# Sliding-window attention followed by an expert layer: Q and K of the first two batches loaded in runs of eight rows, the exponent in key order, new pacing of loads

## The chip, the cores and the metric

The kernel runs on one core of a Trainium2 chip. The metric is the device time of one execution in microseconds. Runs of a kernel are executed in rounds next to runs of the kernel before on the same chip. A "point" is one per cent of the time of the kernel before. TensorE is called PE below, as in the profile; VectorE is DVE, ScalarE is ACT, GpSimd is POOL, and SP is the engine whose queue issues most of the transfers.

## The reference

Eight batches of attention with eight heads, 576 positions and 64 channels, where each position sees only positions at most 32 away. The heads are joined to 4608 tokens of 512 channels, which go through one expert: a matrix product to 2048, the square of the relu with a scale and a bias, and a product back to 512.

```python
scores = scale * np.matmul(q, k.transpose(0, 1, 3, 2))      # q, k: (8, 8, 576, 64) float32, of size 0.1
mask = np.abs(pos[:, None] - pos[None, :]) <= 32
attn = softmax(np.where(mask, scores, -1e9))                # cut: written out with max, exp and sum
x = np.matmul(attn, v).transpose(0, 2, 1, 3).reshape(4608, 512)
r = np.maximum(x @ w_in, 0.0)                               # w_in: (512, 2048)
return (s * (r * r) + b) @ w_out                            # w_out: (2048, 512)
```

## The kernel before

The program is a list of tasks. Each task has a stream (an engine or the SP queue), an estimated cost, an estimated landing time if it is a transfer, a key (the lower, the sooner) and a slack. A list scheduler written in the kernel simulates these estimates when the program is built and fixes the order of the instructions on every engine. Each engine is then given its instructions in that fixed order.

Q and K of batches 0 and 1 are loaded early, cast to bf16, transposed on PE and scattered into two layouts, `QT` for queries and the block-diagonal `KBD` for keys. Batches 2 to 7 use DMA transposes instead, and their loads are paced: they wait for the attention of an earlier unit.

```python
PACE = ((0, 0, 1, 2, 3, 3), (0, 0, 1, 2, 3, 3), (0, 1, 2, 3, 3, 3))   # unit of batch b-1 that a Q/K load of batch b waits for
PACEV = ((0, 0, 1, 1), (0, 0, 1, 1), (0, 1, 2, 2))                     # the same for V

def pairs_chunk(b, name, t0, n, key, load_key, banks, slack=0.0):      # n partitions: 128, 128, 32; two rows each, all heads
    add("sp", lambda e: e.dma_start(
        STG[si][0:n, 0:1024].rearrange("p (h c) -> p h c", h=H),
        src_of[name][b, :, t0:t0 + 2 * n, :].rearrange("h (p i) d -> p h (i d)", i=2)),   # runs of 2 rows = 512 bytes
        600.0, writes=[("STG", si)], key=load_key, dma=("l", n // 2, 30.0))
    # ... cast to NAT, 8 transposes on PE into a PSUM bank, then for q:
    for i in range(2):
        add("act", lambda e, i=i: e.copy(QT[slot][:, i, :, t0 // 2:t0 // 2 + n], view[:, :, i, 0:n]), ...)
    # ... for k: a scatter with a step of two elements into KBD, halves on DVE and ACT

# in unit(b, m): four score products into SC (PSUM), then the exponent of 128x512
src = src.rearrange("p a (i c) -> p a i c", i=2)
add("act", lambda e, src=src, dst=dst: e.activation(
    dst.rearrange("p a (c i) -> p a i c", i=2), src, AF.Exp, bias=0.0, scale=0.125), ...)   # dense read, write with a step of 2

# V of batches from 2 on is issued by POOL, staged in VST, and cast into VBD by DVE and ACT
cast_v(b, due(b, 0) - 4.0, (("dve", "act"), ("dve", "act")), 3000.0)   # 3000 is the slack, in ns

# the order of the first part (cut)
qk(0, 0, 128); qk(0, 256, 128); load_v(0, ...); qk(0, 512, 32)         # then units of batch 0, w_in, w_out (first half)
qk(1, 0, 128); load_v(1, ..., waits=[land["out", 2, 0]]); unit(1, 0)   # then more of batch 1, w_out (second half)
```

The "column sum" that is named below is a product of the output weights with a matrix of ones. It serves the bias `b` and needs all of one half of `w_out`; there are two, one per half. "Expansion" is the product with `w_in`, and an "output sum" is DVE's reading of a finished product with `w_out` (`outs`). A transfer "lands" when its data have arrived. The "granted clock" is the share of full speed at which TensorE ran.

The softmax here doesn't subtract the row's maximum and nothing guards it: scores larger than these inputs give would overflow.

## Time and profile before

| | before |
|---|---|
| time, median of 3 (range) | 335.08 us (334.21 to 335.22) |
| PE busy in the profiled span of 331.1 us | 308.5 us |
| first exponent starts | 11.54 us |
| last V issue of batch 0 ends | 12.64 us |
| first expansion matmul starts | 24.20 us |
| last V issue of batch 1 ends | 49.37 us |
| second column sum starts | 59.67 us |

These are the page's busy totals, with PE's share in 40 slices and the granted clock below (9 stands for 90% or more):

```profile
...
PE 308.5 (93%) x2199; PEld 179.5 (54%) x2234; DVE 206.6 (62%) x485; ACT 166.4 (50%) x270; POOL 87.6 (26%) x136
...
PE   1778998899999999999989999999999999999995
...
PEclk9999999799999999999999999999999999999999
...
```

PE is busy for 93% of the span, and what is missing lies mainly in the first slices. The table by stretches gives this in numbers. Its columns are the stretch, its length, the busy time of each engine with its number of instructions, the granted clock, the DMA engines' busy share, and GB/s (I read a share near or above 1 as full):

```profile
...
core 0: us, PE busy (x) PEld busy (x) DVE busy (x) ACT busy (x) POOL busy (x), PEclk, DMA share, GB/s
0.00:20.00 20.00, 9.50 (x80) 6.86 (x82) 11.87 (x29) 14.45 (x19) 14.50 (x28) 1.00 1.07 238
20.00:40.00 20.00, 17.60 (x252) 16.04 (x250) 12.96 (x27) 12.86 (x24) 7.19 (x7) 1.00 1.10 343
40.00:60.00 20.00, 17.76 (x212) 15.35 (x213) 11.57 (x24) 15.35 (x28) 8.36 (x9) 1.00 1.11 254
60.00:80.00 20.00, 18.84 (x172) 14.38 (x171) 12.38 (x27) 9.05 (x15) 8.17 (x14) 0.92 0.95 213
...
160.00:180.00 20.00, 18.95 (x118) 9.73 (x119) 14.17 (x33) 9.34 (x15) 4.03 (x7) 1.00 0.99 189
...
```

PE is idle for 10.5 us in the first 20 us and for 16.3 us in the first 80. The DMA engines are full in the first 60 us (shares of 1.07 to 1.11), so I take it that the order and speed of transfers decide how fast PE gets going. The SP queue's timeline of the first microseconds shows this. Its columns are start, duration, queue, line, operation, tiles and count; the first issue takes 0.45 us, and I read a much longer one as held up by the transfers ahead of it (the trace gives the durations alone):

```profile
...
start us, us, engine line op out<-in xcount [idle before <-releaser]
0.81 0.45 SPq L456 DMA_DIRECT2D stg<-in_q_dram  x1
...
3.24 1.61 SPq L456 DMA_DIRECT2D stg<-in_k_dram  x1
4.90 7.74 SPq L432 DMA_DIRECT2D vst<-in_v_dram  x8
...
```

The first four loads of Q and K are issued by 4.9 us, but eight V loads then take 7.74 us to issue, as I read it because the transfers ahead of them are still under way. While Q and K land, the table by stretches shows 300 GB/s:

```profile
...
4.00:8.00 4.00, 1.04 (x8) 0.77 (x8) 3.35 (x15) 2.12 (x4) 3.33 (x11) 1.00 1.19 300
...
```

The V loads of batch 1 are issued like this:

```profile
...
40.62 8.75 SPq L432 DMA_DIRECT2D vst<-in_v_dram  x8
...
```

The groups of ACT by shape are next; after the bar stand busy time and the mean of one in ns. The relu writes densely and the exponent with a step of two elements, and a 128x512 costs 598 ns against 743:

```profile
...
L705 ACT ACTIVATE r<-w 128x512 bf16<-128x512 f32 x144 | 85.4, 598 | 95.0 <-PE w L698 80.8 <-DVE outs L730 11.3 <-DVE gt L707 2.0
L560 ACT ACTIVATE exo<-sc 128x512 bf16<-128x512 f32 x32 | 23.8, 743 | 4.8 <-PE sc L543 4.6
...
```

Last, PE's timeline around the second column sum (the brackets give the idle time just before, and what ended it). PE waits 1.34 us for an output sum and then does the column sum in 3.33 us. The first column sum takes 1.91 us. This one runs at half the clock: the granted clock was 0.50 from 59.96 to 63.38, for 3.42 us:

```profile
...
58.78 0.61 PE L717 MATMUL o<-wout,gt 128*128 128x256 bf16 x4 [1.34 <-DVE outs L730]
...
59.67 3.33 PE L740 MATMUL o<-wout,onesw 128*128 128x256 bf16 x16
...
```

### The profile page before, as it was taken

The page shows a single profiled execution, that of the slowest core. Times are in us where ns is not written, and L with a number is a line of the kernel's source. Part 1 is how long each engine was busy: PE and PEld are TensorE (multiplying, and loading weights), DVE is VectorE, ACT ScalarE, POOL GpSimd, SP SyncE. Part 2 cuts the span into 40 slices and gives each one's busy share as a digit, 9 for nine tenths or more (in the row PEclk, how much of TensorE's full clock was granted, in tenths as well). Part 3 has the DMA queues.
Part 4 walks back from the last instruction along what each step waited for, and adds up shares of the span by engine and source line. Part 5 has one row for each costly group of instructions (what it writes and reads, how often), then busy time and mean ns, then how long its engine had stood idle before and what let it go on. Part 6 is the DMA issues. An engine that isn't in the chain of part 4 may idle for free.

```text
span 331.1 us, 5839 instructions
## 1 busy us (share of the span) xinstructions
PE 308.5 (93%) x2199; PEld 179.5 (54%) x2234; DVE 206.6 (62%) x485; ACT 166.4 (50%) x270; POOL 87.6 (26%) x136
## 2 busy tenths in 40 slices
PE   1778998899999999999989999999999999999995
PEld 1567996775554555456445555555455544444442
DVE  6556564269777776898578768765874453323411
ACT  6696497229552664657175655444644433333300
POOL 8562443830910226044205500450000000000000
PEclk9999999799999999999999999999999999999999
DMA  8999999899999699979998996999811111000021
GB/s 211 224 363 357 295 195 297 219 241 167 209 202 197 193 195 206 230 170 245 173 228 163 225 212 145 247 169 213 146 56 54 56 46 62 35 32 34 32 93 68
DMA packets 107836, 57.15 MB, mean 173 GB/s; under 512 B 56608, under 2 KB 100128, under 8 KB 107808
## 3 DMA queue, kind: packets, MB, share of 16 engines
q1 hardware_dynamic: 103200, 49.69, 68.7%
q0 software_dynamic: 4608, 7.08, 11.3%
q8 instruction: 17, 0.28, 0.4%
q14 instruction: 11, 0.09, 0.1%
HBM read 36.70 MB, written 9.44 MB: 139 GB/s over the span
## 4 chain that ended last, share of the span: by engine, by line
PE 70%; DMA 13%; SPq 8%; POOL 3%; DVE 2%; ACT 2%; issue 2%; ACTq 0%
PE o L717 31%; PE w L698 29%; PE avn L582 6%; SPq L432 5%; DMA vst<-in_v_dram 5%; PE sc L543 3%; DMA stg<-in_moe_w_in_dram 3%; DMA stg<-in_moe_w_out_dram 3%; POOL vst L432 2%; SPq L456 2%; DMA out_dram<-outs 2%; ACT vbd L445 1%; SPq L416 1%; PE o L740 1%; DVE vbd L446 0%
## 5 line engine op out<-in xcount | busy, mean ns | idle before, releaser
L717 PE MATMUL o<-wout,gt 128*128 128x512 bf16 (+1 forms) x629 | 140.4, 357 | 1.9 <-DVE outs L730 1.3
L698 PE MATMUL w<-xt,win 128*128 128x512 bf16 (+2 forms) x685 | 139.8, 339 | 2.2 <-ACT r L705 1.2
L705 ACT ACTIVATE r<-w 128x512 bf16<-128x512 f32 x144 | 85.4, 598 | 95.0 <-PE w L698 80.8
L707 DVE TENSOR_TENSOR gt<-r 128x512 bf16<-128x512 bf16 x144 | 61.3, 432 | 55.1 <-ACT r L705 54.4
L717 PEld LDWEIGHTS o<-wout,gt 128*128 128x128 bf16 x640 | 61.1, 98 | 59.7 <-DVE outs L730 2.0
L698 PEld LDWEIGHTS w<-xt,win 128*128 128x128 bf16 x704 | 61.6, 98 | 52.4 <-ACT r L705 1.8
L432 POOL DMA_DIRECT2D vst<-in_v_dram x96 | 59.4, 626 | 106.8 <-PE avn L582 57.7
L730 DVE SCALAR_TENSOR_TENSOR outs<-o,sb,cvec 128x512 f32<-128x512 f32 (+1 forms) x40 | 27.7, 692 | 18.6 <-PE o L717 16.2
L560 ACT ACTIVATE exe<-sc 128x512 bf16<-128x512 f32 (+1 forms) x40 | 27.5, 687 | 15.7 <-PE sc L543 15.1
L582 PE MATMUL avn<-vbd,exo 128*128 128x130 bf16 (+1 forms) x240 | 27.9, 221 | 1.5 <-ACT xt L607 1.3
L595 DVE TENSOR_TENSOR xn<-avn,rec 128x512 bf16<-128x512 f32 (+1 forms) x38 | 26.1, 686 | 3.2 <-DMA xt<-xn 2.5
L543 PE MATMUL sc<-qt,kbd 128*128 128x128 bf16 (+1 forms) x288 | 24.8, 220 | 1.6 <-ACT exe L560 1.1
L582 PE MATMUL avn<-vbd,exe 128*128 128x130 bf16 (+1 forms) x152 | 25.3, 221 | 1.0 <-ACT vbd L445 1.0
L560 ACT ACTIVATE exo<-sc 128x512 bf16<-128x512 f32 x32 | 23.8, 743 | 4.8 <-PE sc L543 4.6
L543 PEld LDWEIGHTS sc<-qt,kbd 128*128 128x128 bf16 x288 | 20.5, 100 | 9.9 <-issue 1.0
L445 ACT CAST vbd<-vst 64x1024 bf16<-64x1024 f32 (+1 forms) x15 | 16.5, 1139 | 17.5 <-DMA vst<-in_v_dram 17.5
L582 PEld LDWEIGHTS avn<-vbd,exo 128*128 128x128 bf16 (+1 forms) x240 | 22.0, 105 | 5.5 <-ACT xt L607 1.6
L506 DVE CAST nat<-stg 128x1024 bf16<-128x1024 f32 (+1 forms) x36 | 23.7, 680 | 0.0
L521 DVE COPY kbd<-kt 64x512 bf16<-64x512 bf16 (+1 forms) x72 | 19.1, 266 | 0.8
L582 PEld LDWEIGHTS avn<-vbd,exe 128*128 128x128 bf16 (+1 forms) x152 | 16.1, 109 | 4.3 <-ACT vbd L445 1.4
L446 DVE CAST vbd<-vst 64x1024 bf16<-64x1024 f32 (+1 forms) x16 | 11.7, 745 | 7.3 <-DMA vst<-in_v_dram 7.3
L564 DVE TENSOR_TENSOR exe<-exe,mask 128x512 bf16<-128x512 bf16 (+1 forms) x30 | 11.7, 391 | 7.1 <-ACT exe L560 7.0
(63 smaller groups left out, 133.3 us busy)
## 6 DMA issues: line engine op xcount, KB each, us to landing
stg<-in_q_dram SPq DMA_DIRECT2D x16, 512.0 KB, 5.5
stg<-in_k_dram SPq DMA_DIRECT2D x16, 512.0 KB, 7.2
out_dram<-outs SPq DMA_DIRECT2D x32, 256.0 KB, 2.6
vst<-in_v_dram POOLq DMA_DIRECT2D x96, 72.0 KB, 5.5
stg<-in_moe_w_in_dram SPq DMA_DIRECT2D x8, 512.0 KB, 8.7
stg<-in_moe_w_out_dram SPq DMA_DIRECT2D x8, 512.0 KB, 8.3
vst<-in_v_dram SPq DMA_DIRECT2D x16, 144.0 KB, 4.7
stg<-in_q_dram SPq DMA_DIRECT2D x8, 128.0 KB, 6.2
```

The costliest lines, as they stand in the source:

```text
L432: add(stream, lambda e, dst=dst, src=src: e.dma_start(dst, src), 640.0 if stream == "sp" else 700.0, writes=[("VST", h, x) for x in (range ...
L445: add(eng, (lambda e, dst=dst, src=src: e.copy(dst, src)) if eng == "act" else (lambda e, dst=dst, src=src: e.tensor_copy(dst, src)), {"ac ...
L506: add("dve", lambda e, si=si, ni=ni: e.tensor_copy(NAT[ni][0:n, :, :].rearrange("p i (h d) -> p h i d", h=H), STG[si][0:n, 0:1024].rearran ...
L543: fns = [lambda e, j=j, pr=pr, lo=lo, hi=hi, w=w, par=par: e.matmul(SC[:, par, pr * 128:pr * 128 + w], lhsT=KBD[:, pr, j, :], rhs=QT[slot] ...
L560: add("act", lambda e, src=src, dst=dst: e.activation(dst.rearrange("p a (c i) -> p a i c", i=2), src, AF.Exp, bias=0.0, scale=0.125), 190 ...
L582: fns.append(lambda e, pr=pr, buf=buf, col=col, j=j, x=x, last=len(parts) - 1: e.matmul(av[0:nr, pr, 0:130], lhsT=buf[:, pr, col:col + nr] ...
L595: add("dve", lambda e: e.tensor_tensor(XN[xi][0:nr, :].rearrange("p (a b c) -> p a b c", a=4, b=2), av[0:nr, :, 0:128].rearrange("p a (b c ...
L698: add("pe", [lambda e, g=g, kc=kc: e.matmul(wt[:, g, :], lhsT=WIN_BF[:, kc, (f0 + g) * 128:(f0 + g + 1) * 128], rhs=XT[:, kc, t0 % XR:t0 % ...
L705: add("act", lambda e: e.activation(rt, wt, AF.Relu, bias=0.0, scale=1.0), 190 + 0.833 * 512, reads=[("W", wb)], writes=[("R1", rb)], key=key)
L707: add("dve", lambda e: e.tensor_tensor(GT[gs][:, f0:f0 + ng, g0:g0 + nt], rt, rt, ALU.mult), 130 + 0.53 * 512, reads=[("R1", rb)], writes= ...
L717: add("pe", [lambda e, fc=fc: e.matmul(O[:, ob, 0:cn], lhsT=GT[gs][:, fc, g0:g0 + 128], rhs=WOUT_BF[:, fc, c0:c0 + cn], start=(fc == 0), s ...
L730: add("dve", lambda e: e.scalar_tensor_tensor(OUTS[us][:, 0:cn], O[:, ob, 0:cn], SB128[:, 0:1], CVEC[:, c0:c0 + cn], ALU.mult, ALU.add), 2 ...
```

## The change

The intent: Q and K of the first two batches are read in runs of eight rows per head pair, so that a contiguous piece has 2 KB in place of 512 bytes and there are eight loads per batch of 72 partitions each. Eight-row runs change the order of queries and keys, so the exponent now reads PSUM with a step and writes densely. All loads of the first part are held in strict order, and the pacing of later loads is eased.

```diff
+ROWS = 8
-PACE = ((0, 0, 1, 2, 3, 3), (0, 0, 1, 2, 3, 3), (0, 1, 2, 3, 3, 3))
-PACEV = ((0, 0, 1, 1), (0, 0, 1, 1), (0, 1, 2, 2))
+PACE = ((-1, -1, -1, 0, 1, 1), (-1, -1, 0, 1, 2, 2), (0, 0, 1, 2, 3, 3))
+PACEV = ((-1, -1, -1, -1), (0, 0, 0, 0), (0, 1, 2, 2))          # -1: one unit earlier, in batch b-2
... (the scheduler: tasks with key < -100 are chained in the order in which they are added)
-        NSTG, NNAT, NEX, ... = 9, 6, 3, ...
+        NSTG, NNAT, NEX, ... = 9, 5, 4, ...
... (weight casts)
-                key=key + 20.0, slack=100.0)
+                key=key + 150.0, slack=100.0)
-        def pairs_chunk(b, name, t0, n, key, load_key, banks, slack=0.0):
+        def load_pair(b, name, pr, key, load_key, banks, eng, slack):
+            n = S // ROWS                                              # 72
             add("sp", lambda e: e.dma_start(
-                STG[si][0:n, 0:1024].rearrange("p (h c) -> p h c", h=H),
-                src_of[name][b, :, t0:t0 + 2 * n, :].rearrange("h (p i) d -> p h (i d)", i=2)),
-                600.0, writes=[("STG", si)], key=load_key, dma=("l", n // 2, 30.0))
+                STG[si][0:n, :].rearrange("p (h c) -> p h c", h=2),
+                src_of[name][b, 2 * pr:2 * pr + 2, :, :].rearrange("h (p i) d -> p h (i d)", i=ROWS)),
+                600.0, writes=[("STG", si)], key=load_key, dma=("l", 9, 86.0))
... (eight 72x128 transposes per load, one copy into QT, or two into KBD)
-                src = src.rearrange("p a (i c) -> p a i c", i=2)
+                src = src.rearrange("p a (i c) -> p a c i", i=nrow)    # nrow: 8 for b < 2, else 2
-                    dst.rearrange("p a (c i) -> p a i c", i=2), src, AF.Exp, bias=0.0, scale=0.125),
+                    dst.rearrange("p a (c i) -> p a c i", i=nrow), src, AF.Exp, bias=0.0, scale=0.125),
... (order of the first part: all Q, K of a batch, then its V, then its units; V of batch 1 no longer waits for w_out)
-                load_v(1, h, nxt(), "sp", waits=[land["out", 2, 0]])
+                load_v(1, h, nxt(), "sp")
```

The term `("l", 9, 86.0)` tells the scheduler that such a load keeps the transfer engines for 9 times 86 ns, that is 0.77 us. A load has 72 times 4 KB.

## The prediction

> **What bounds it now.** The tensor engine: the busy table gives PE 308.5 of 331.1 us. The table by stretches shows PE idle 10.5 us in 0–20, 2.4 in 20–40, 2.1 in 50–60, 1.2 in 70–80, 2.2 in 100–260 and 3.8 at the end. At 60–63 the granted clock is 0.50; the second column sum takes 3.33 us against 1.91 for the first. Only these gaps can be won, and the change touches those of the first 90 us.
>
> **Head.** The timeline shows V issued at 4.9–12.6 (0.97 us per load), the DMA engines saturated, V cast at 15.7–19.2, ACT busy almost throughout, and the first expansion matmul at 24.2. Q and K in 512-byte packets move at about 290 GB/s, V in 256-byte packets at 205, weights in 2 KB packets at 390.
>
> - Runs of eight make the packets 2 KB; at 390 GB/s that saves 2 us per batch. But a load now has 72 partitions. [...] Loads before have 128, 64 or 32 partitions, so no run here shows this yet.
> - All eight loads must land before the first score: the first exponent moves from 11.5 to about 15 us. It was not the limit; V and ACT were.
> - ACT: an exponent with strided writes takes 0.74 us per 128x512, a relu with contiguous ones 0.60; a K scatter 0.65, a contiguous Q copy 0.53. So each exponent saves about 0.12 us, and the head about 1.5 us of ACT. Transposes become 64 instead of 48 per batch (+1 us of PE in batch 1).
> - Sum: first expansion matmul at about 23.2, 1 us earlier.
>
> **Middle.** Strict load order and fewer descriptors (Q, K issues of 2.5–3.4 us in the queue's timeline shrink to about 0.5) should bring V of batch 1 from 52 us to about 46 and the second half of w_out from 58 to about 52. That would remove the idle time at 54 and 57–59 and perhaps the half clock after it, 3–4 us. Against it: on POOL the sixteen V issues of batch 2 (0.63 us each, 10 us) now stand before all four w_out casts (1.04 each), and wait for the V casts of batch 1. So the second column sum can't start before about 62 us, while PE arrives at about 60. I expect PE to wait for POOL there for 1–4 us, again followed by some 3.4 us of half clock[...]. Most of the gain here is lost.
>
> **Later.** Batch 2 is loaded some 10 us sooner, so the 1.2 us of idle time at 73–76 goes. Steady blocks stay PE bound; shorter exponents there are off the critical path.
>
> **Sum.** −1 head, −1 middle, −1 batch 2, +0.5 transposes: 335.1 to about 332.5 us; range 328.7–335.5. Chances: faster by over 2% 0.09, within 2% 0.89, slower 0.02.
>
> **What would show it.** Q, K loads at 290 GB/s[...]; exponents near 0.62 us; first expansion matmul near 23; PE waiting for POOL before the second column sum, clock 0.5 after it; no gap at 73–76.
>
> **What would make it wrong.** [...] Strided PSUM reads slower than strided writes, or PE's fixed order waiting for batch 1's transposes: 336.

Passages are cut where marked: how a load of 72 partitions would be split over the transfer engines, the rate that I worked out from it, a case of 327–329 us that presupposed it, and a rule of when the full clock returns. The step from the head ended in no gain from the longer packets: I put the Q and K loads at 290 GB/s, their rate in the trace of before (5 to 8 us). The sum came to −1 −1 −1 +0.5, that is −2.5 us, from 335.1 to 332.6, given as about 332.5; the head's −1 counts nothing for faster loads because of that step. The 3.4 us of half clock are the stretch from 59.96 to 63.38 in the trace of before.

## The result, and the profile after

The changed kernel takes 352.38 us in the median of 4 runs (351.46 to 356.85, the longest slow), and the kernel before 334.64 us (333.97 to 335.22) beside it. The ratio is 1.0521, with a 95% interval from 1.0477 to 1.0566. A ratio is the mean time of one kernel's runs over that of the other's of the same rounds, so it is not quite the ratio of the medians. Executions over 1.5% slower than the fastest of the same kernel are left out of the means. The results are correct. The prediction of 332.5 us, with a range up to 335.5, was wrong.

| | before | after |
|---|---|---|
| time, median of the same rounds | 334.64 us | 352.38 us |
| profiled span, granted clock | 331.1 us, 0.993 | 349.9 us, 0.985 |
| PE busy / idle (span less busy) | 308.5 / 22.6 us | 313.3 / 36.6 us |
| ACT busy | 166.4 us | 159.2 us |
| first exponent starts | 11.54 us | 18.83 us |
| last V issue of batch 0 ends | 12.64 us | 17.24 us |
| first expansion matmul starts | 24.20 us | 26.90 us |
| last V issue of batch 1 ends | 49.37 us | 55.49 us |
| second column sum starts | 59.67 us | 73.20 us |

The same views of the changed kernel follow. The page's totals and slices:

```profile
...
PE 313.3 (90%) x2231; PEld 180.5 (52%) x2266; DVE 204.3 (58%) x485; ACT 159.2 (46%) x262; POOL 88.6 (25%) x138
...
PE   1487879949999999999599998999999999999996
...
```

PE gained 14.0 us of idle time and 4.8 us of busy time, and the work is nearly the same, so slower matmuls at a lower clock (a mean of 0.985 against 0.993) are the likely source of the latter. The table by stretches:

```profile
...
0.00:20.00 20.00, 7.07 (x76) 5.22 (x78) 11.13 (x29) 10.35 (x13) 12.60 (x27) 1.00 0.87 182
20.00:40.00 20.00, 16.41 (x218) 13.72 (x217) 10.72 (x21) 12.64 (x22) 6.80 (x6) 1.00 1.01 336
40.00:60.00 20.00, 16.78 (x190) 13.50 (x190) 10.93 (x22) 10.79 (x17) 6.13 (x7) 0.91 0.84 193
60.00:80.00 20.00, 14.80 (x167) 12.39 (x167) 8.68 (x19) 10.58 (x18) 12.96 (x19) 1.00 1.16 269
...
160.00:180.00 20.00, 15.60 (x85) 7.76 (x85) 10.48 (x22) 7.36 (x11) 4.88 (x8) 0.83 1.18 187
...
```

The columns are those of before. PE is idle for 24.9 us in the first 80 us, 8.6 more than before. Another 3.4 us comes between 160 and 180, where the clock is also at 0.83. In the first 20 us the DMA share is 0.87 and not 1.07, and the rate 182 GB/s and not 238. The SP queue and the rate while Q and K land:

```profile
...
0.81 0.43 SPq L476 DMA_DIRECT2D stg<-in_q_dram  x1
...
3.86 0.40 SPq L476 DMA_DIRECT2D stg<-in_k_dram  x1
4.30 12.94 SPq L448 DMA_DIRECT2D vst<-in_v_dram  x8
...
```

```profile
...
4.00:12.00 8.00, 2.81 (x35) 2.12 (x36) 4.07 (x10) 3.83 (x6) 4.18 (x10) 1.00 0.90 200
...
```

All eight loads are issued by 4.3 us, as the change intended. But they move at only 200 GB/s at a share of 0.90, and the V issues behind them take 12.94 us. For batch 1:

```profile
...
40.56 14.93 SPq L448 DMA_DIRECT2D vst<-in_v_dram  x8
...
```

V of batch 1 begins to be issued at the same time as before, and ends 6 us later. The exponent and relu:

```profile
...
L567 ACT ACTIVATE exo<-sc 128x512 bf16<-128x512 f32 x32 | 19.1, 598 | 2.5 <-PE sc L550 2.5
...
```

The exponent now costs what the relu costs (598 ns in this kernel too). Around the second column sum:

```profile
...
73.20 1.92 PE L744 MATMUL o<-wout,onesw 128*128 128x256 bf16 x16 [0.45 <-POOL wout L431]
...
78.48 2.36 PE L721 MATMUL o<-wout,gt 128*128 128x256 bf16 x20 [2.68 <-DVE outs L734]
...
```

It starts 13.5 us later than before. Its wait for POOL is just 0.45 us, and its clock is full. After it comes a wait for output sums of 2.68 us. The late stall is seen in PE's timeline, then DVE's, then in the table by stretches:

```profile
...
175.35 0.34 PE L589 MATMUL avn<-vbd,exo 128*96 128x130 bf16 x1 [4.29 <-DVE exe L571]
...
```

```profile
...
174.01 0.69 DVE L462 CAST vbd<-vst 64x1024 bf16<-64x1024 f32 x1 [2.87 <-DMA vst<-in_v_dram]
174.62 0.41 DVE L711 TENSOR_TENSOR gt<-r 128x512 bf16<-128x512 bf16 x1
174.95 0.34 DVE L571 TENSOR_TENSOR exe<-exe,mask 128x384 bf16<-128x384 bf16 x1
...
```

```profile
...
175.20:180.00 4.80, 4.65 (x17) 2.26 (x18) 3.10 (x7) 2.20 (x2) 0.00 (x0) 0.50 1.27 223
...
```

PE needs the masked exponent, which is DVE's multiply at 174.95. Ahead of it in DVE's order stands a V cast at 174.01, which had itself waited for V to land. PE does nothing for 4.29 us and then works at a clock of 0.50. The sixteen V transfers that the cast needs took, from issue to landing:

```profile
...
DMA to landing us min/median/max: 4.5/10.3/11.3
```

### The profile page after: what moved, and what is told of

It is laid out like the page before. It is cut to its first block, busy times and chain, and to the rows that moved or that the text cites. A ratio compares the mean times of both kernels' runs of the same rounds, so it can differ in the third digit from the quotient of the medians.

```text
span 349.9 us, 5916 instructions
## 1 busy us (share of the span) xinstructions
PE 313.3 (90%) x2231; PEld 180.5 (52%) x2266; DVE 204.3 (58%) x485; ACT 159.2 (46%) x262; POOL 88.6 (25%) x138
## 4 chain that ended last, share of the span: by engine, by line
PE 67%; DMA 19%; SPq 4%; POOL 3%; DVE 3%; issue 2%; ACT 1%; ACTq 0%
PE o L721 31%; PE w L702 27%; DMA vst<-in_v_dram 7%; PE avn L589 5%; DMA stg<-in_k_dram 4%; SPq L448 3%; PE sc L550 3%; DMA out_dram<-outs 3%; DMA stg<-in_moe_w_out_dram 3%; POOL vst L448 3%; DMA xt<-xn 2%; SPq L476 1%; DVE xn L602 1%; DVE outs L734 0%; ACT r L709 0%
## 5 line engine op out<-in xcount | busy, mean ns | idle before, releaser
L721 PE MATMUL o<-wout,gt 128*128 128x512 bf16 (+1 forms) x627 | 143.7, 361 | 5.8 <-DVE outs L734 2.7
L702 PE MATMUL w<-xt,win 128*128 128x512 bf16 (+2 forms) x686 | 142.3, 342 | 2.3 <-ACT r L709 1.4
L711 DVE TENSOR_TENSOR gt<-r 128x512 bf16<-128x512 bf16 x144 | 60.1, 424 | 59.3 <-ACT r L709 58.6
L702 PEld LDWEIGHTS w<-xt,win 128*128 128x128 bf16 x704 | 62.7, 99 | 55.2 <-ACT r L709 2.3
L734 DVE SCALAR_TENSOR_TENSOR outs<-o,sb,cvec 128x512 f32<-128x512 f32 (+1 forms) x40 | 27.6, 691 | 22.6 <-PE o L721 19.3
L567 ACT ACTIVATE exe<-sc 128x512 bf16<-128x512 f32 (+1 forms) x40 | 22.1, 553 | 13.1 <-PE sc L550 13.0
L567 ACT ACTIVATE exo<-sc 128x512 bf16<-128x512 f32 x32 | 19.1, 598 | 2.5 <-PE sc L550 2.5
L599 DVE RECIPROCAL rec<-avn 128x8 f32<-128x8 f32 (+1 forms) x38 | 7.7, 202 | 15.8 <-PE avn L589 15.6
```

The lines of the kernel that those rows point to most:

```text
L567: add("act", lambda e, src=src, dst=dst: e.activation(dst.rearrange("p a (c i) -> p a c i", i=nrow), src, AF.Exp, bias=0.0, scale=0.125), ...
L702: add("pe", [lambda e, g=g, kc=kc: e.matmul(wt[:, g, :], lhsT=WIN_BF[:, kc, (f0 + g) * 128:(f0 + g + 1) * 128], rhs=XT[:, kc, t0 % XR:t0 % ...
L711: add("dve", lambda e: e.tensor_tensor(GT[gs][:, f0:f0 + ng, g0:g0 + nt], rt, rt, ALU.mult), 130 + 0.53 * 512, reads=[("R1", rb)], writes= ...
L721: add("pe", [lambda e, fc=fc: e.matmul(O[:, ob, 0:cn], lhsT=GT[gs][:, fc, g0:g0 + 128], rhs=WOUT_BF[:, fc, c0:c0 + cn], start=(fc == 0), s ...
L734: add("dve", lambda e: e.scalar_tensor_tensor(OUTS[us][:, 0:cn], O[:, ob, 0:cn], SB128[:, 0:1], CVEC[:, c0:c0 + cn], ALU.mult, ALU.add), 2 ...
```

## The experiments

**Theory A**: loads on 72 partitions are slow, not only because they keep fewer transfer engines busy (a share of 0.83 between 4 and 8 us, where the kernel before has 1.19) but because nearly all their rows lie in one half of SBUF. The second part was an assumption, which the first run below tests. **Theory B**: the plan, made with wrong landing times, places V casts ahead of work that PE needs. **Rivals**: the new pacing, the strict order of loads, the new exponent, and the order of weight casts on POOL. Where full-rate loads are named, the casts read zeros.

### Rates of load shapes alone

A kernel that only loads: groups of eight loads, each group waited for before the next; its output is wrong. It is one run, and its state is unknown.

```diff
+groups = [pair(t, 0, 72, 0), pair(t, 0, 64, 0), pair(t, 0, 64, 64), pair(t, 0, 64, 64 * (t % 2)), pair(t, 0, 72, 28),
+          flat(t, 80), flat(t, 96), flat(t, 128), two(t, 72), two(t, 128),        # pair(load, first row, rows, first partition)
+          pair(t, 0, 64, 0) + pair(t, 64, 8, 64), pair(t, 0, 32, 0) + pair(t, 32, 8, 64) + pair(t, 40, 32, 72)]
```

> Loads alone, wrong result on purpose: twelve groups of eight loads, each group waited for to the end, all from DRAM on the SP queue. Theory E (engines[...]): 72 rows in partitions 0-71 about 205 GB/s, the same 72 rows in partitions 28-99 about the same 205[...], 64 rows in 0-63 faster than 72[...], 80 rows in 0-79 near 290 or more. Theory P (the side of the SBUF: 64 of the 72 rows go into the lower 64 partitions[...]): 72 rows in 28-99 clearly faster, 280 or more; 64 rows in 0-63 no faster than about 210, and the same in 64-127; 64 rows alternating between the halves, and 96 and 128 rows, faster, up to 390. Rival R (2 KB runs with a stride are slow whatever the partitions): all 2 KB groups near 205. 512-byte packets at 128 rows: 290.

Theory E is that 72 rows keep only a part of the transfer engines busy, Theory P that the half of SBUF counts.

The table by stretches, one stretch per group; the lines below are 72 rows in partitions 0 to 71, 64 in 0 to 63, 64 in 64 to 127, 64 in alternate halves, 72 in 28 to 99, then 80, 96 and 128 rows from partition 0, and the last is each load cut into 32, 8 and 32 rows:

```profile
...
4.00:11.00 7.00, 0.00 (x0) 0.00 (x0) 1.00 0.80 212
17.00:23.50 6.50, 0.00 (x0) 0.00 (x0) 1.00 1.07 211
29.50:36.00 6.50, 0.00 (x0) 0.00 (x0) 1.00 1.08 217
41.50:46.50 5.00, 0.00 (x0) 0.00 (x0) 1.00 1.06 237
53.00:59.50 6.50, 0.00 (x0) 0.00 (x0) 1.00 0.79 243
64.00:70.00 6.00, 0.00 (x0) 0.00 (x0) 1.00 1.06 249
77.00:83.00 6.00, 0.00 (x0) 0.00 (x0) 1.00 1.05 275
90.00:98.00 8.00, 0.00 (x0) 0.00 (x0) 1.00 0.97 344
...
153.00:160.50 7.50, 0.00 (x0) 0.00 (x0) 1.00 1.06 204
...
```

Two limits are seen. 64 rows occupy all engines (share 1.07) and yet reach only 211 GB/s in one half of SBUF and 217 in the other, against 237 in alternate halves and 344 for 128 rows: lying in one half goes with a low rate by itself. And 72 rows in 28 to 99, which lie in both halves, reach 243 at a share of 0.79: not all engines are busy with them. From the shares I estimate three quarters of the engines (0.79 of the 1.07 that 64 rows show is 0.74), which would be twelve of the sixteen that the page counts. 72 rows at 0 to 71 have both limits (share 0.80) and reach 212. The lower share alone thus goes with less than the prediction allowed: 243 GB/s, where it had about 290. Why it is not three quarters of the 344 of 128 rows, an estimate of 258, is open. With 512-byte packets 72 rows reach 181, and 128 rows 295. Eighty rows reach 249, 96 rows 275, and the cut into 64 and 8 rows 224. So the run length did buy something, and the 72 partitions cost more than that.

### Each load cut over both halves

```diff
-            add("sp", lambda e: e.dma_start(STG[si][0:n, :]..., rows), ...)
+            add("sp", [lambda e: e.dma_start(into[0:32], rows[0:32]),
+                       lambda e: e.dma_start(into[64:72], rows[32:40]),
+                       lambda e: e.dma_start(into[72:104], rows[40:72])], ...)
```

The casts read a tile of zeros here, with unchanged waits, as the rows land in other partitions. The result still passes the comparison, I take it because scores of inputs of size 0.1 are so small that zero scores stay within the tolerance; it is not the reference's computation.

> The kernel after, with each Q, K load cut into three so that 32 rows land in partitions 0-31 and 40 in 64-103 (the casts read zeros: wrong result on purpose; order of everything else the same). If the slow loads are the cause (main theory): Q, K move at 300 GB/s or more, first exponent at about 14 us instead of 18.8, first expansion matmul at about 23.5 instead of 26.5, second column sum at about 63 instead of 73, time 337 to 342. If the new order and pacing are the cause (rival): 348 or more.

Measured: 346.21 us, ratio 1.0354 (1.0326 to 1.0382). The expectation missed: the loads moved at 225 GB/s between 4 and 11 us, nearer to the 204 of the run above than to 300 or more. The edit did not do what it was made for, so it is no test of Theory A, though the loads were a little faster and the kernel 1.7 points faster than the changed one. The run of load shapes could have warned me: loads of 64 rows in alternate halves reached 237 GB/s against 211, just 12% more.

### The pacing of before

```diff
-PACE = ((-1, -1, -1, 0, 1, 1), (-1, -1, 0, 1, 2, 2), (0, 0, 1, 2, 3, 3))
+PACE = ((0, 0, 1, 2, 3, 3), (0, 0, 1, 2, 3, 3), (0, 1, 2, 3, 3, 3))     # PACEV likewise
```

> The kernel after with the pacing tables of before. Main theory (loads): the first 80 us stay as slow; only the 4.3 us stall at 171-175 and the half clock after it may go, and V of batch 2 no longer stands before the w_out casts: 343 to 349. Rival (pacing): 338 or less.

Measured: 347.79 us, ratio 1.0383 (1.0348 to 1.0418). The start stays slow (first expansion matmul at 27.01). But the second column sum comes at 65.49 and not 73.20, and PE is busy for 58.75 of the first 80 us and not 55.06 (63.70 before); the late stall shrinks to 1.54 us. So the pacing has a share in both.

### The loads and layout of before inside the changed kernel

```diff
-ROWS = 8
+ROWS = 2                       # and load_pair is replaced by pairs_chunk of before, in the changed kernel's order
```

> The kernel after with the loads and the layout of before (512-byte packets, 128 rows), but its order of loads, exponent and pacing. Main theory (loads): first expansion matmul at 23 to 24.5 us, V of batch 1 lands by 48, 334 to 341. Rival (order and pacing): 346 or more.

Measured: 340.30 us, ratio 1.0176 (1.0147 to 1.0205), with right results. The first expansion matmul comes at 24.78. About two thirds of the loss is gone: 1.0521 less 1.0176 is 3.45 points, or 11.5 us of 333.5. It undoes the layout together with the loads, so it is not yet clean.

### The same plan with loads at full rate

The same bytes of each load are spread over 128 partitions, in 128 runs of 2304 bytes and not 144 of 2048, which is to lift both limits at once (128 rows reached 344 GB/s alone). The planner's estimates stay, so the plan stays (the planner of both kernels, run without the chip, gives the same order on all five engines). The casts read zeros, so the data are wrong. The casts are no faster for that: on POOL, single casts of Q took 1.42 and 1.53 us in the two later runs with the same edit (full rate and the pacing of before, and later V casts), against 1.04 in the changed kernel.

```diff
-                STG[si][0:n, :].rearrange("p (h c) -> p h c", h=2),
-                src_of[name][b, 2 * pr:2 * pr + 2, :, :].rearrange("h (p i) d -> p h (i d)", i=ROWS)),
+                STG[si][:, 0:576],
+                src_of[name][b, 2 * pr:2 * pr + 2, :, :].rearrange("h s d -> (h s d)").rearrange("(p c) -> p c", p=128)),
```

> The kernel after with the same eight loads per batch, the same bytes and the same plan, but each load spread over 128 partitions (the casts read zeros, so the scores are wrong on purpose). Alone, 128 rows of 2 KB moved at 340 to 370 GB/s, 72 rows in 0-71 at 212. Main theory (rate of the 72-row loads): Q, K land by 9 to 10 us instead of 15.3, first expansion matmul at 22 to 23.5 instead of 26.9, V of batch 1 cast by 47, time 336 to 341, i.e. most of the 18 us gone. Rival (order and pacing): 346 or more.

Measured: 339.50 us, ratio 1.0179 (1.0125 to 1.0232): 3.4 points, or 11.4 us. The rate while Q and K land, and V's issues behind them:

```profile
...
4.00:8.00 4.00, 1.32 (x16) 0.98 (x16) 2.99 (x9) 2.44 (x4) 3.59 (x7) 1.00 0.97 303
...
```

```profile
...
4.80 8.46 SPq L449 DMA_DIRECT2D vst<-in_v_dram  x8
...
```

303 GB/s in place of 200, and V's issues take 8.46 us and not 12.94. The first expansion matmul comes at 23.61 and not 26.90, and the second column sum at 63.84 and not 73.20. This settles the larger part: it is the rate of the 72-partition loads, twice, with all that queues behind them. A stall of 4.68 us remains in PE, with the same cause in DVE's timeline as before: a V cast that waited for its data, with the mask multiply behind it.

```profile
...
164.93 0.68 DVE L463 CAST vbd<-vst 64x1024 bf16<-64x1024 f32 x1 [3.10 <-DMA vst<-in_v_dram]
...
165.88 0.34 DVE L572 TENSOR_TENSOR exe<-exe,mask 128x384 bf16<-128x384 bf16 x1
...
```

### Full rate and the pacing of before

```diff
 (full rate as above)
+PACE, PACEV as in the kernel before
```

> As the run before, with the pacing tables of before. If load rate and pacing add up: 331 to 336, near or under the kernel before. If the strict load order, or waiting for all eight loads before the first score, costs by itself: 338 or more.

Measured: 340.92 us, ratio 1.0242 (1.0188 to 1.0296). The two repairs do not add; the interval overlaps that of full rate alone. The stall moved from 162 to 78 us (4.36 us of PE), again with a V cast ahead in DVE's order that had waited 5.02 us for its data. So here the pacing of before gains nothing and only moves the stall, where in the changed kernel it gained 1.4 points.

### Two-row loads and the pacing of before

```diff
 (loads and layout of before as above)
+PACE, PACEV as in the kernel before
```

> The kernel after with two-row loads (512-byte packets, 128 rows) and the pacing tables of before; its strict load order and its exponent are kept. If loads and pacing are the two causes: 333 to 337. If strict order costs by itself: 338 or more, with PE waiting in 40-80 us.

Measured: 336.93 us, ratio 1.0098 (1.0042 to 1.0154). Results are right. With two-row loads the pacing of before gains 0.8 points. What remains of the change in this kernel is the order of the first part, the keys of the weight casts and of some first fills, the buffers and the exponent.

### The new exponent alone in the kernel before

```diff
-                src = src.rearrange("p a (i c) -> p a i c", i=2)
+                src = src.rearrange("p a (i c) -> p a c i", i=2)
-                    dst.rearrange("p a (c i) -> p a i c", i=2), src, AF.Exp, ...
+                    dst.rearrange("p a (c i) -> p a c i", i=2), src, AF.Exp, ...
```

> The kernel before with one part of the change alone: the exponent reads PSUM with a stride and writes runs. The order of instructions is the same as before on every engine. Exponents of 128x512 fall from 0.74 to 0.60 us, ACT busy time by about 9 us; time 333.5 to 335 (0 to 1 us less), because ACT is off the chain after 25 us. Rival (ACT holds back PE throughout): 331 or less.

Measured: 331.42 us beside 332.93, ratio 0.9971 (0.9925 to 1.0016). ACT's busy time falls from 166.4 to 159.7 us, and the time by at most a fraction of a per cent that is not told from nothing.

### Later V casts, with full rate

The slack of the V casts of batches from 2 on goes from 3000 to 8000 ns, so that the scheduler lets other ready work go first.

```diff
-cast_v(b, due(b, 0) - 4.0, (("dve", "act"), ("dve", "act")), 3000.0)
+cast_v(b, due(b, 0) - 4.0, (("dve", "act"), ("dve", "act")), 8000.0)
```

> The run with loads at full rate and the new pacing, with one number changed: the plan keeps 8 instead of 3 us of reserve between the landing of V and its cast, so the V casts of batches 2 to 7 stand later in the queues of DVE and ACT. Theory (what is left of the loss after the loads are repaired comes from V casts that stand in front of DVE work which PE needs, and wait for a late V): the 4.7 us stall at 162-166 and the half clock after it go, 332 to 336. Rival (the rest comes from the strict order or the late w_out casts): 338 or more.

Measured: 333.60 us, ratio 1.0035 (0.9969 to 1.0101): equal to the kernel before within the interval. The stretch of the late stall, in the table by stretches:

```profile
...
160.00:180.00 20.00, 19.89 (x130) 10.74 (x132) 16.28 (x42) 10.70 (x18) 4.82 (x8) 1.00 0.84 193
...
```

PE is busy for 19.89 of 20 us, against 15.60 in the changed kernel.

### Later V casts in the changed kernel, otherwise untouched

> The kernel after with that same number changed and nothing else. If slow loads and V casts in the way add up: the stall at 171-175 goes, 345 to 349, the first 80 us as slow as in the kernel after. If the loads were all of it: 351 to 353.

The edit is the one above, in the changed kernel. Measured: 343.79 us, ratio 1.0331 (1.0266 to 1.0397), slightly better than expected. PE is again busy for 19.89 us between 160 and 180. With the three runs before it this gives a table of two by two:

| | V casts as in the change | V casts later |
|---|---|---|
| 72-partition loads | 1.0521 | 1.0331 |
| loads at full rate | 1.0179 | 1.0035 |

The loads are worth 3.4 or 3.0 points, the V casts 1.9 or 1.4. Both together account for 4.9 of 5.2 points. (Each ratio is against the kernel before in its own rounds; the four do not all come from the same rounds.)

### No strict order of loads

```diff
-        after = [self.chain] if key < -100 and self.chain else []
+        after = []
```

> The kernel after without the strict order of the first loads (each load goes when its buffer is free in the plan). Main theory: the order is not what costs, 349 to 354. Rival (strict order blocks the queue behind buffers): 345 or less.

Measured: 354.90 us, ratio 1.0638 (1.0587 to 1.0689), about one point slower than with it (other rounds; the intervals do not meet), and just above the expectation. The strict order is not the cause; if anything it helps.

### A candidate: new exponent and one more output buffer in the kernel before

```diff
 (exponent as above)
-        NSTG, NNAT, NEX, NXN, NR1, NOUT, XR = 9, 6, 3, 2, 3, 3, 2048
+        NSTG, NNAT, NEX, NXN, NR1, NOUT, XR = 9, 6, 3, 2, 3, 4, 2048
```

> A candidate to beat both: the kernel before with the new exponent, and four output buffers instead of three, because before and with the exponent alone PE waits 1.3 to 1.9 us at 57-59 for an output buffer whose store is queued behind V. Expected: that wait goes, 328.5 to 331.5 where before is 333 to 335. If another wait takes its place: as with the exponent alone, 331 to 334.

Measured: 337.62 us, ratio 1.0100 (1.0049 to 1.0151); the profiled run was slow. The expectation missed. In its trace the wait for output sums before the column sum is gone, but the plan came out differently and has a wait of 3.95 us at 240 us for a mask multiply, some work after a V cast that waited 3.37 us for its data. As this is a slow run, no time is laid to it.

### The old order of the exponent in the changed kernel

```diff
-                src = src.rearrange("p a (i c) -> p a c i", i=nrow)
+                src = src.rearrange("p a (i c) -> p a i c", i=nrow)
-                    dst.rearrange("p a (c i) -> p a c i", i=nrow), src, AF.Exp, ...
+                    dst.rearrange("p a (c i) -> p a i c", i=nrow), src, AF.Exp, ...
```

> The changed kernel with the exponent's old order (contiguous read, scattered write). If the exponent's cost is off the path there, as it was in the kernel before, this is within 0.5% of the changed kernel, 1.050 to 1.058 of before; if the faster exponent gains inside the changed kernel, 1.06 or more.

Measured: 363.69 us, ratio 1.0911 (1.0864 to 1.0957), 3.9 points slower than the changed kernel. So the exponent's new order is worth about 13 us inside the change, where in the kernel before it is worth next to nothing. The reason is in ACT's groups by shape between 19 and 80 us:

```profile
...
L567 ACT ACTIVATE exo<-sc 128x512 bf16<-128x512 f32 x7 | 18.2, 2606 | 0.0
...
```

With eight-row runs the dense read makes a write with a step of eight elements, 16 bytes, and a 128x512 costs about 2.6 us, not 0.60. ACT is then busy for 19.93 us between 20 and 40. The new order is a condition of the eight-row layout, not an extra gain beside it.

### Two-row loads and later V casts

```diff
 (loads and layout of before as above; slack of V casts 8000)
```

> The changed kernel with the loads of before (two-row layout) and the later V casts; it gives right results. If slow loads and V casts placed too early are together all of the loss, this ends at 0.995 to 1.005 of before (it was 1.018 with the loads alone). If a third cost is still in the changed order or pacing, it stays at 1.012 or more.

Measured: 336.48 us, ratio 1.0095 (1.0059 to 1.0130), with right results. This lies between the two expectations. Late V casts help here too (1.0176 to 1.0095), but one per cent stays.

### The new exponent and later V casts in the kernel before

```diff
 (exponent as above; slack of V casts 8000)
```

> The kernel before with the new exponent and the later V casts. If late V casts are a gain in themselves, 0.985 to 0.993 of before. If they only mend what the changed kernel's plan broke, the same as with the exponent alone, 0.995 to 1.000.

Measured: 333.79 us, ratio 1.0031 (0.9985 to 1.0076). This lies a little above both expectations. Late V casts are no gain in themselves; they mend what the changed plan broke.

### Weight casts ahead of the V issues on POOL

In the changed kernel the sixteen V issues of batch 2 stand before all four casts of the second half of `w_out`; in the kernel before, the casts stand first. This was my third suspect. One number puts them first again, in three kernels: with two-row loads, in the changed kernel, and at full rate (wrong data); all three with later V casts.

```diff
-                key=key + 150.0, slack=100.0)
+                key=key + 100.0, slack=100.0)
```

> Loads of before, later V casts, and the output-weight casts put ahead of the 16 V issues of batch 2 in GpSimd's order, as they were in the kernel before; right results. If that order is the third cost, the second column sum starts by 62 us at full clock (66.65 at half clock without it) and the time is 0.993 to 1.003 of before. If not, it stays at 1.006 or more.

> The changed kernel with only these two plan repairs, its 72-row loads kept; right results. If the weight casts behind V issues cost it the same 0.5 to 1 per cent, 1.020 to 1.029 of before (1.033 without). If its slow loads hold the column sum back anyway, 1.03 or more.

> The changed kernel with loads of full rate (same bytes, wrong data on purpose) and both plan repairs. If the eight-row route is worth anything once loads are fast, 0.985 to 0.998 of before (1.0035 without the weight casts first); if it has no gain left, 1.000 or more.

| | without | weight casts first |
|---|---|---|
| two-row loads | 1.0095 | 1.0101 (1.0065 to 1.0137) |
| the changed kernel | 1.0331 | 1.0462 (1.0417 to 1.0508) |
| full rate | 1.0035 | 1.0132 (1.0081 to 1.0183) |

The medians are 336.45, 348.69 and 338.64 us. All three hopes failed. With two-row loads the edit did what it was made for, as PE's timeline shows: the second column sum starts at 60.27 (66.65 without) at full clock. And the time is the same. The plan that came of it has another wait, again for a mask multiply, and just ahead of that in DVE's order stands a copy of K that waited for its DMA transpose (the last line is DVE's):

```profile
...
60.27 1.92 PE L755 MATMUL o<-wout,onesw 128*128 128x256 bf16 x16 [0.60 <-POOL wout L431]
...
90.54 0.23 PE L603 MATMUL avn<-vbd,exo 128*128 128x130 bf16 x1 [2.76 <-DVE exo L585]
...
89.24 0.80 DVE L542 COPY kbd<-kt 64x128 bf16<-64x128 bf16 x4 [3.78 <-DMA kt<-nat]
...
```

By 70 us PE has done 631 matmuls here and 606 without the edit, by 94 us 775 and 805. So a lead, counted in matmuls, was won and lost again, and these runs do not show what the late column sum costs by itself. The copy of K is a suspect that no run tests: without the edit DVE waits 2.95 us for one at 117.7 to 120.7, and PE then 2.05 us for work behind it. The kernel before has no such wait among DVE's. The last per cent in the kernels with right results is not settled.

## Why the prediction was wrong

1. **"Q, K loads at 290 GB/s", no gain from longer packets.** This is the step that failed; how it came about is cut from the prediction. It named one limit, and there were two. That only a part of the engines is busy was right: the share is 0.80 in the run of load shapes, and 1.07 with 64 rows. But its rate was too high even so (243 GB/s with both halves), and 72 partitions from 0 lie nearly all in one half of SBUF: the loads reached 212 GB/s alone and 200 in the kernel, below the 290 to 300 of before. I took them as equal and so booked a loss of 11 us as zero; slower loads were not among the things that I said would make it wrong. V in the trace of before moved at 205 GB/s on 64 partitions (10 to 13 us), which may have been a hint. It does not tell the half from the packets of 256 bytes: V's loads alternate between the halves, and loads that do so reached 237 with 2 KB packets.
2. **"The first exponent moves from 11.5 to about 15 us. It was not the limit; V and ACT were."** It moved to 18.83, and V with it: V queues behind Q and K. "First expansion matmul at about 23.2" came at 26.90; at full rate it came at 23.61.
3. **"Should bring V of batch 1 from 52 us to about 46."** Its issue ended at 55.49 and its first cast began at 57.34 (52.38 before). At full rate the issue ended at 45.66 and the cast began at 47.94, so the reasoning of order was sound and its input was not.
4. **The order on POOL** was read rightly, and its cost wrongly. "PE to wait for POOL there for 1–4 us" was 0.45, as PE itself arrived late, and the clock after it was full (1.00 from 73 to 84 us). Putting the casts first gained nothing in three kernels.
5. **"Exponents near 0.62 us"** was right: 0.60. So was that they are off the critical path in later blocks. What I did not see is that the eight-row layout would cost 2.6 us per exponent without them.
6. **"Steady blocks stay PE bound"** failed: 4.29 us of idle time at 171 to 175 and half the clock after it, until 180.1: about 4.8 us of busy time, where the prediction counted on 3.4 from the trace of before. The runs with later V casts show that V casts placed ahead of needed work cost 5 to 6 us (1.4 to 1.9 points of 333.5). The plan places them so because it believes V to land sooner. In the kernel's text a V transfer with nothing else under way lands 700 + 700 + 1.125 times 370 + 1100 ns after its issue, 2.9 us, and the planner, run without the chip, has 2.9 us for all sixteen transfers ahead of the stall; the trace has up to 11.3. A cast waits in the plan for that landing, 0.1 us and the slack: 6.0 us after the issue, or 11.0 with the slack of 8000. Why V took so long to land there was not tested.
7. **"No gap at 73–76"** failed: a gap of 2.68 us at 75.8 to 78.5, on output sums.

The cause of 4.9 of 5.2 points is shown, with loads whose data are not used. How much of the loads' share is due to the half and how much to the lower share of busy engines is seen in the run of load shapes alone, not inside the kernel. Open is why kernels with right results and both repairs stay 1% above before. Nothing that I ran beats the kernel before beyond its interval.

## What to carry to other kernels

When a layout change alters how many partitions a load covers, ask both what share of the DMA engines it keeps busy (here 0.79 with 72 rows in both halves, 1.07 with 64) and which part of SBUF it reaches (72 rows: 212 GB/s at 0 to 71, 243 at 28 to 99), and measure that one load alone before trusting the longer packet. In a kernel whose order is fixed by a planner, a wrong landing time costs twice, once where the data come late and again where the engine stands waiting in front of work that was ready. A cheap repair of one visible wait is worth trying, but count the whole span, because the plan may move the wait elsewhere.
